# Causal attention feeding a hard-swish MLP on one core: the order of every queue from a list scheduler written into the kernel

## The chip, the cores and the metric

One core of a Trainium2 chip. Times are device microseconds of one execution. Engines are named as the profile names them: PE is TensorE (its matmuls; PEld is its weight loads), DVE is VectorE, ACT is ScalarE, POOL is GpSimd, SP is the engine that issues all DMAs here. Each engine takes its instructions in the order in which the program lists them.

## The reference

Attention with a causal mask over 4 batches, 12 heads, 448 positions and a head size of 64, then a hard-swish MLP over the 1792 tokens (768 to 2048 to 768), all in float32:

```python
scores = scale * np.matmul(q, k.transpose(0, 1, 3, 2))
scores = np.where(mask, -1000000000.0, scores)
scores = scores - np.max(scores, axis=-1, keepdims=True)
attn = np.exp(scores)
attn = attn / (np.sum(attn, axis=-1, keepdims=True) + 1e-09)
out = np.matmul(attn, v)            # heads joined: x is 1792 x 768
h = x @ w_in
g = h * np.clip(h + 3.0, 0.0, 6.0) / 6.0
return g @ w_out
```

## The kernel before

The tokens are handled in five groups. Group 0 holds the first 112 positions of all four batches (448 columns); groups 1 to 4 hold the other 336 positions of one batch each.

**Attention.** Two heads, a pair, are worked on together. For group 0 there are six pairs (`scores_first`, `transposed_first`, `times_v_first`), and their outputs come before any MLP work of group 0. For groups 1 to 4 there are 24 pairs, six a group, each in three kinds of PE work: scores (`scores`, L221, tile `s` from `kr`,`qr`; three row blocks of 448, 336 and 224 columns for each of the two heads), 18 transposes of the normalised probabilities (`transposed`, L250, `s` from `ident`,`pr`), and the product with V (`times_v`, L268, `av` from `pt`,`vr`; widths 336, 336, 224, 112 for each head). The scores of one head use 64 rows of the PE array and the other head the other 64 rows, so the two matmuls of a pair of heads can run side by side; the products with V use 64 columns each in the same way. These are called tiled matmuls below. Everything else on PE uses the whole array. Before the transposes, DVE adds the mask and takes the maximum (L224), ACT takes exponentials (L228), DVE inverts the sums (L236, L237), and POOL scales the probabilities (`norm`, L240; L172 in group 0).

**MLP.** Each product of float32 operands is made of three matmuls on a high and a low part (`wh`, `wl`, `xh`, `xl`, `gh`, `gl`; L334 to L336 for the first layer, L355 to L357 for the second). A group takes 288 matmuls for each layer, 576 in all. Weights come in 40 chunks a group. In group 0 a chunk is first put together from two interleaved halves by three DVE operations (L312, L313, L314, tile `wf`), written to a scratch tensor `kept_w`, and split by ACT (`wh`, L84) and POOL (`wl`, L89). In later groups it is read back from `kept_w` and split by ACT and DVE.

**Order.** Each step is given a time number by hand (`at(t, fn, ...)`), the steps are traced in the order of these numbers, and the framework's own scheduler then places the instructions of all engines, instruction by instruction. PSUM has five banks for `s`, one for `av`, two for `mo`.

Of the kernel before, what the change touches and what calls it, by code (L numbers as in the profile page):

```python
# [17 lines left out]

# [1 line left out]

# [23 lines left out]
T_FIRST, T_REST, T_LOAD, T_PT, T_AV, T_W, T_WLOAD = -66, -22, -20, 9, 16, 7, 7  # L44
# [3 lines left out]
def tile_causal_attention_hardswish_moe(ctx: ExitStack, tc: tile.TileContext, q, k, v, w_in, w_out, out):  # L48
# [5 lines left out]
    pools = {}  # L54

    def pool(name, bufs, **kw):
        pools[name] = ctx.enter_context(tc.tile_pool(name=name, bufs=bufs, **kw))

    def mk(tag, shape, dt=F32):
        return pools[tag].tile(shape, dt, tag=tag, name=tag)  # L60

    def bank(tag):
        return mk(tag, [128, 512])

    pool("const", 1)
    pool("gh", 1)
    pool("gl", 1)
    for tag in ("prow", "wf", "r", "ob"):
        pool(tag, 2)
    for tag in ("qr", "kr", "vr", "wh", "wl"):  # L70
        pool(tag, 3)
    for tag in ("pr3", "pr2", "pr1", "pt0", "pt1", "pt2", "wd"):
        pool(tag, 4)
    for tag in ("xh", "xl"):
        pool(tag, 9)
    for tag, bufs in (("s", 5), ("av", 1), ("mo", 2)):
        pool(tag, bufs, space=bass.MemoryType.PSUM)
# [35 lines left out]
    steps = []  # L113

    def at(t, fn, *a):
        steps.append((t, len(steps), fn, a))

    x_t = {}

    def x_split(g, p, x, n):  # L120
        xh, xl = mk("xh", [128, S], F32R)[:, :n], mk("xl", [128, S], F32R)[:, :n]
        x_t[g, p] = xh, xl
        nc.scalar.copy(xh, x)
        nc.vector.tensor_tensor(xl, x, f(xh), ALU.subtract)  # L124


    first, fprob, fpt = {}, {}, {}

    def load_first(p):
        if p == 0:  # L130
            first["qk"] = mk("gh", [128, 2 * NPAIR, S])
            first["v"] = mk("gl", [128, NPAIR, S + 64])
        for a, src in enumerate((q, k)):
            nc.sync.dma_start(
                out=first["qk"][:, 2 * p + a].rearrange("m (b s) -> m b s", b=B),
                in_=src[:, p, :, :, :C].rearrange("b e d s -> (e d) b s"),
            )
        first["ld", p] = nc.sync.dma_start(
            out=first["v"][:C, p].rearrange("c (b e d) -> c b (e d)", b=B, e=2),
            in_=v[:, p, :, 0].rearrange("b c e d -> c b (e d)"),  # L140
        )

    def scores_first(p):
        qa, ka = (first["qk"][:, 2 * p + a].rearrange("m (b s) -> m b s", b=B) for a in range(2))
        st = mk("prow", [C, 2, 8])
        banks = [bank("s") for _ in range(2)]
        ps = [t[:C, :S].rearrange("c (b s) -> c b s", b=B) for t in banks]
        pr = [mk("pr3", [C, S]).rearrange("c (b s) -> c b s", b=B) for _ in range(2)]
        for e in range(2):
            nc.tensor.matmul(ps[e], identr, maskr, start=True, stop=False)  # L150
        for b in range(B):
            for e in range(2):
                r = slice(64 * e, 64 * e + 64)
                nc.tensor.matmul(ps[e][:, b], qa[r, b], ka[r, b], start=False, stop=b == B - 1)
        for e in range(2):
            nc.vector.tensor_reduce(st[:, e, :4], ps[e], AX.X, ALU.max)
        nc.vector.tensor_scalar(st[:, 1, :4], st[:, 1, :4], -0.125, None, ALU.mult)
        for b in range(B):
            nc.scalar.activation(
                pr[1][:, b], ps[1][:, b], ACTF.Exp, bias=st[:, 1, b:b + 1], scale=0.125,  # L160
                accum_out=st[:, 1, 4 + b:5 + b],
            )
        nc.vector.tensor_tensor(
            pr[0], ps[0], st[:, 0, :4].unsqueeze(2).to_broadcast([C, B, C]), ALU.subtract
        )
        nc.scalar.activation(pr[0], pr[0], ACTF.Exp, scale=0.125)
        nc.vector.tensor_reduce(st[:, 0, 4:], pr[0], AX.X, ALU.add)
        r = st[:, :, 4:8]
        nc.vector.tensor_scalar_add(r, r, 1e-9)
        nc.vector.reciprocal(r, r)  # L170
        for e in range(2):
            nc.gpsimd.tensor_tensor(  # L172
                pr[e], pr[e], st[:, e, 4:].unsqueeze(2).to_broadcast([C, B, C]), ALU.mult
            )
        fprob[p] = pr

    def transposed_first(p, e):
        ps, ph = bank("s"), mk("pt0", [C, S])
        for b in range(B):
            nc.tensor.transpose(ps[:C, C * b:C * b + C], fprob[p][e][:, b], ident)  # L180
        if e:
            nc.vector.tensor_copy(ph, ps[:C, :S])
        else:
            nc.scalar.copy(ph, ps[:C, :S])
# [261 lines left out]
```

## Time and profile before

| | us |
|---|---|
| median of 3 runs (lowest, highest) | 727.09 (725.49, 728.04) |
| profiled execution, its own time | 725.93 |
| span of that execution, first to last instruction | 724.2 |
| PE busy (share of the span) | 700.4 (97%) |
| PEld busy | 579.1 (80%) |
| DVE busy | 455.1 (63%) |
| ACT busy | 343.1 (47%) |
| POOL busy | 211.8 (29%) |

PE's matmuls overlap one another in the trace: a matmul of 336 columns is shown as some 320 ns long while the next one starts some 155 ns after it. So PE's busy time doesn't say how much PE could be pressed together; starts that follow one another do. A float32 matmul that is not split into parts by hand shows as two instructions in the trace (8 rows for 4 matmuls).

### The profile page before, as it was taken

The numbers are of one execution on the slowest core, as the hardware profiler recorded it, in microseconds if no ns is written. First come the engines' busy times: TensorE is split into PE (matmuls) and PEld (weight loads), VectorE is DVE, ScalarE is ACT, GpSimd is POOL, SyncE is SP. The second block draws the span as 40 slices with busy tenths as digits, with TensorE's granted clock in tenths as the row PEclk, the third lists the DMA queues.
The fourth block names the chain that finished last, engine by engine and source line by source line (L and its number), as shares of the span: only waits on it lengthen the run. The fifth ranks groups of instructions, "written<-read, shape, count | busy, mean of one in ns | idle before, by whom it ended". The sixth has DMA issues, their size and how long they took to land.

```text
span 724.2 us, 11850 instructions
## 1 busy us (share of the span) xinstructions
PE 700.4 (97%) x4236; PEld 579.1 (80%) x4236; DVE 455.1 (63%) x907; ACT 343.1 (47%) x801; POOL 211.8 (29%) x266
## 2 busy tenths in 40 slices
PE   5889998999999999999999999999999999999998
PEld 4656865877766887788887789888888789999998
DVE  5784999888787666554556665445575653466432
ACT  3346454553343555454555454455555544444432
POOL 1543544434645241222220433211243212011100
PEclk9878999899999999999999999999999999999999
DMA  9971574466787543244564334545442234654452
GB/s 242 305 263 49 183 278 148 145 215 215 253 278 228 167 131 107 72 143 147 149 178 122 105 98 123 145 140 157 146 141 76 62 100 123 197 157 125 129 163 72
DMA packets 60347, 113.63 MB, mean 157 GB/s; under 512 B 14976, under 2 KB 26880, under 8 KB 60288
## 3 DMA queue, kind: packets, MB, share of 16 engines
q1 hardware_dynamic: 60288, 112.88, 51.6%
q8 instruction: 33, 0.54, 0.3%
q14 instruction: 26, 0.21, 0.1%
HBM read 94.77 MB, written 18.09 MB: 156 GB/s over the span
## 4 chain that ended last, share of the span: by engine, by line
PE 80%; DVE 10%; issue 3%; DMA 3%; POOL 2%; ACT 1%; SPq 1%; POOLq 0%; ACTq 0%; DVEq 0%
PE mo L334 11%; PE mo L355 10%; PE mo L336 10%; PE mo L335 10%; PE mo L357 9%; PE mo L356 9%; PE s L221 7%; PE av L268 7%; PE s L250 5%; DVE wf L313 2%; DVE wf L314 2%; DVE wf L312 2%; DVE gl L89 1%; DMA wd<-in_w_in_dram 1%; DMA kept_w<-wf 1%
## 5 line engine op out<-in xcount | busy, mean ns | idle before, releaser
L89 DVE TENSOR_TENSOR wl<-wd,wh 128x512 fp32r<-128x512 f32 (+1 forms) x160 | 132.3, 827 | 122.8 <-ACT wh L84 119.9
L84 ACT CAST wh<-wd 128x512 fp32r<-128x512 f32 (+1 forms) x160 | 112.8, 705 | 131.9 <-PE mo L356 66.6
L334 PE MATMUL mo<-xh,wh 128*128 128x336 f32 (+1 forms) x480 | 166.4, 348 | 1.7 <-DVE r L342 1.7
L355 PE MATMUL mo<-gh,wh 128*128 128x336 f32 (+1 forms) x480 | 165.6, 345 | 0.0
L357 PE MATMUL mo<-gh,wl 128*128 128x336 f32 (+1 forms) x480 | 158.6, 331 | 1.5 <-POOL wl L89 1.5
L336 PE MATMUL mo<-xh,wl 128*128 128x336 f32 (+1 forms) x480 | 159.1, 331 | 0.0
L335 PE MATMUL mo<-xl,wh 128*128 128x336 f32 (+1 forms) x480 | 158.4, 330 | 0.2 <-DVE xl L124 0.2
L356 PE MATMUL mo<-gl,wh 128*128 128x336 f32 (+1 forms) x480 | 157.6, 328 | 0.0
L240 POOL TENSOR_SCALAR pr<-pr,prow 112x224 f32<-112x224 f32 x144 | 99.9, 713 | 149.4 <-DVE prow L237 113.6
L228 ACT ACTIVATE pr<-s,prow 112x448 f32<-112x448 f32 (+1 forms) x144 | 77.3, 540 | 106.3 <-DVE prow L224 106.3
L334 PEld LDWEIGHTS mo<-xh,wh 128*128 128x128 f32 x480 | 91.0, 190 | 23.9 <-issue 12.7
L355 PEld LDWEIGHTS mo<-gh,wh 128*128 128x128 f32 x480 | 90.3, 188 | 17.5 <-issue 13.5
L224 DVE CUSTOM_DVE_ANT_0 s<-s,mask 112x448 f32<-112x448 f32 (+1 forms) x144 | 71.7, 522 | 42.2 <-PE s L221 42.1
L86 POOL TENSOR_SCALAR gh<-r 128x336 fp32r<-128x336 f32 x64 | 33.7, 527 | 207.7 <-DVE r L342 206.3
L335 PEld LDWEIGHTS mo<-xl,wh 128*128 128x128 f32 x480 | 91.5, 191 | 3.2 <-issue 1.3
L357 PEld LDWEIGHTS mo<-gh,wl 128*128 128x128 f32 x480 | 90.2, 188 | 4.4 <-POOL wl L89 1.9
L336 PEld LDWEIGHTS mo<-xh,wl 128*128 128x128 f32 x480 | 91.3, 190 | 2.5 <-issue 0.9
L89 POOL TENSOR_TENSOR wl<-wf,wh 128x512 fp32r<-128x512 f32 (+1 forms) x40 | 66.1, 1659 | 88.2 <-ACT wh L84 85.5
L356 PEld LDWEIGHTS mo<-gl,wh 128*128 128x128 f32 x480 | 90.5, 189 | 1.0
L221 PE MATMUL s<-kr,qr 64*112 64x224 f32 (+2 forms) x288 | 69.3, 503 | 1.4 <-ACT pr L228 1.4
L250 PE MATMUL s<-ident,pr 112*112 112x112 f32 x432 | 63.0, 260 | 1.1 <-POOL pr L240 0.8
L89 DVE TENSOR_TENSOR gl<-r,gh 128x336 fp32r<-128x336 f32 (+1 forms) x80 | 50.2, 630 | 21.5 <-POOL gh L86 20.4
(52 smaller groups left out, 685.4 us busy)
## 6 DMA issues: line engine op xcount, KB each, us to landing
wd<-kept_w SPq DMA_DIRECT2D x64, 384.0 KB, 3.1
wd<-kept_w SPq DMA_DIRECT2D x96, 256.0 KB, 2.6
wd<-in_w_in_dram SPq DMA_DIRECT2D x16, 768.0 KB, 4.9
wd<-in_w_out_dram SPq DMA_DIRECT2D x24, 512.0 KB, 5.0
kept_w<-wf SPq DMA_DIRECT2D x16, 384.0 KB, 2.6
kept_w<-wf SPq DMA_DIRECT2D x24, 256.0 KB, 2.9
kr<-in_k_dram SPq DMA_DIRECT2D x24, 224.0 KB, 3.4
vr<-in_v_dram SPq DMA_DIRECT2D x24, 224.0 KB, 2.7
```

The lines of the kernel that those rows point to most:

```text
L84: nc.scalar.copy(o, i)
L89: (nc.gpsimd if eng == "P" else nc.vector).tensor_tensor(o, a, b, ALU.subtract)
L221: nc.tensor.matmul(dst[e], qr[r, C * (i - 1):C * i], kr[r, :w], start=True, stop=True)
L228: nc.scalar.activation(prob[n][e, i], dst[e], ACTF.Exp, bias=st[:, e, i:i + 1], scale=-1.0, accum_out=st[:, e, 4 + i:5 + i],)
L240: nc.gpsimd.tensor_scalar(pr[e, i], pr[e, i], r[:, e, i - 1:i], 1.0, ALU.mult, ALU.mult)
L250: nc.tensor.transpose(ps[:C, o:o + C], pr[e, i][:, C * j:C * j + C], ident)
L334: nc.tensor.matmul(ps, wh[:, c], xh, start=(c == 0), stop=False)
L335: nc.tensor.matmul(ps, wh[:, c], xl, start=False, stop=False)
L336: nc.tensor.matmul(ps, wl[:, c], xh, start=False, stop=(c == NK - 1))
L355: nc.tensor.matmul(ps, wh[:, j], gh[:, i, :n], start=(i == 0), stop=False)
L356: nc.tensor.matmul(ps, wh[:, j], gl[:, i, :n], start=False, stop=False)
L357: nc.tensor.matmul(ps, wl[:, j], gh[:, i, :n], start=False, stop=(i == NF - 1))
```

## The change

The hand-made list of steps goes away. The kernel now describes each piece of work as an operation with the engines that can do it, assumed durations, what it reads and writes, and which buffers it holds. A list scheduler (`Flow`) plays the five queues through with these numbers, picks an engine where there are several, and its result is emitted in that order under a manual schedule, so that the framework no longer reorders anything. Each tiled operation is now one indivisible piece: the scores of the row blocks 448 and 336 together, those of 224 by themselves, and all eight products with V of a pair of heads in one run. Copies, casts and subtractions that had one engine may go to ACT, DVE or POOL. In the first part the transposed blocks use `mo` banks, the sums of each of the two heads are inverted by themselves, and `prow` has three buffers. All counts of matmuls, transposes, weight operations and DMAs stay as they were.

```diff
-T_FIRST, T_REST, T_LOAD, T_PT, T_AV, T_W, T_WLOAD = -66, -22, -20, 9, 16, 7, 7
+T_FIRST, T_REST, T_LOAD, T_W, T_WLOAD = -66, -22, -24, 9, 9
...
+class Flow:
+    LATENCY = 0.2
+    SWITCH = 0.2
+    DMA_RATE, DMA_LATENCY = 280e3, 1.9
...
+            for e, cand in lists.items():
+                if busy[e] > now + 1e-9:
+                    continue
+                cand[:] = [a for a in cand if a[1].ends is None]
+                for _, o in cand:
+                    need = {}
+                    for b in o.bufs:
+                        if not b.held:
+                            need[b.tag] = need.get(b.tag, 0) + 1
+                    if all(self.free[t] >= n for t, n in need.items()):
+                        self.start(o, e, now, need, out, busy, post)
+                        break
...
+        if e == "PE" and o.tiled != self.mode:
+            t += self.SWITCH / 2
+            self.mode = o.tiled
...
+        move(key, n, lambda: ap(xh)[:, :n], lambda: ap(av)[:, :n], [(av, 0)], [(xh, 0)], {"A": 1, "D": (1, .5)})
...
-        for e in range(2):
-            for i in range(1, NC_):
-                nc.gpsimd.tensor_scalar(pr[e, i], pr[e, i], r[:, e, i - 1:i], 1.0, ALU.mult, ALU.mult)
...
+                one(
+                    t + 4.5 + .1 * e, {"P": 1}, (C * (i + 1) + 300) / 1100, scaled,
+                    [(st, e, 4 + i)], [(pr[e, i], 0)],
+                )
...
+        for j, tiles in enumerate(((3, 2), (1,))):
+            pe(
+                t + 2 * j,
+                [((1.68 * C * (i + 1) + 170) / 1000, lambda i=i: products(i), [(ps[0, i], 0), (ps[1, i], 0), ("turn",)])
+                 for i in tiles],
+                [(qr, 0), (kr, 0)], True,
+            )
...
-        at(t + T_AV, times_v, n, (0, 1))
-        at(t + T_AV + 1, times_v, n, (2, 3))
+        pe(t + 13, [(1.9, times_v, [(av, 0)])], [(vr, 0)] + [(x[0], 0) for x in pt.values()], True)
...
-        rnd("A", wh, w)
-        sub("D" if g else "P", wl, w, f(wh))
+        move(t - T_W + .1, n, lambda: ap(wh)[:, :n], w, [wk], [(wh, 0)], {"A": 1})
+        minus(
+            t - T_W + .2, n, lambda: ap(wl)[:, :n], w, lambda: f(ap(wh))[:, :n], [wk, (wh, 0)], [(wl, 0)],
+            {"D": 1.15, "P": (2, .5)} if g else {"P": 2, "D": (1.15, 2.0)},
+        )
...
-    steps.sort(key=lambda s: s[:2])
-    setup()
-    for _, _, fn, a in steps:
-        fn(*a)
+    order = flow.run()
+    setup()
+    with tc.manual_schedule():
+        for _, _, e, emit in order:
+            emit(e)
```

What stands in the queues now, at three places. First PE in group 1, where a pair's products with V (`av`) and the next pair's scores (`s` from `kr`,`qr`) stand among the MLP's matmuls (`mo`). Before:

```order
L268 MATMUL av<-pt_3721,vr 64x336
L221 MATMUL s<-kr,qr 112x448 x2
L355 MATMUL mo<-gh,wh 128x336
L356 MATMUL mo<-gl,wh 128x336
L357 MATMUL mo<-gh,wl 128x336
L355 MATMUL mo<-gh,wh 128x336
L356 MATMUL mo<-gl,wh 128x336
L357 MATMUL mo<-gh,wl 128x336
L268 MATMUL av<-pt_3685,vr 64x224
L268 MATMUL av<-pt_3736,vr 64x224
L268 MATMUL av<-pt_3685,vr 64x112
L268 MATMUL av<-pt_3736,vr 64x112
```

Now, at a pair's products with V in the same group:

```order
L496 MATMUL av<-pt_2940,vr 64x336
L496 MATMUL av<-pt_2989,vr 64x336
L496 MATMUL av<-pt_2970,vr 64x336
L496 MATMUL av<-pt_3011,vr 64x336
L496 MATMUL av<-pt_2973,vr 64x224
L496 MATMUL av<-pt_3013,vr 64x224
L496 MATMUL av<-pt_2973,vr 64x112
L496 MATMUL av<-pt_3013,vr 64x112
```

The eight products that stood in two parts with six whole-array matmuls between them are one run now. Over the whole program PE changes between whole-array, row-tiled and column-tiled work 275 times before and 162 times now: 109 and 64 times up to the end of group 0, 60 and 36 times in each of groups 1 and 2, 46 and 26 times in group 3. Runs of transposes go from 133 to 91.

Second, PE while the six pairs of group 0 are worked on (L192 before and L394 now are their products with V, L180 and L381 their transposes, L154 and L324 their scores). Before, in the middle of that part:

```order
L334 MATMUL mo<-xh,wh 128x448
L335 MATMUL mo<-xl,wh 128x448
L192 MATMUL av<-pt_346,gl 64x112
L180 MATMUL s<-ident,pr_313 112x112 x3
L192 MATMUL av<-pt_353,gl 64x112
L192 MATMUL av<-pt_346,gl 64x112
L192 MATMUL av<-pt_353,gl 64x112
L192 MATMUL av<-pt_346,gl 64x112
L192 MATMUL av<-pt_353,gl 64x112
L192 MATMUL av<-pt_346,gl 64x112
L192 MATMUL av<-pt_353,gl 64x112
L180 MATMUL s<-ident,pr_313 112x112
```

Now, at the first pair's products:

```order
L394 MATMUL av<-pt_282,gl 64x112
L394 MATMUL av<-pt_266,gl 64x112
L394 MATMUL av<-pt_282,gl 64x112
L394 MATMUL av<-pt_266,gl 64x112
L394 MATMUL av<-pt_282,gl 64x112
L394 MATMUL av<-pt_266,gl 64x112
L394 MATMUL av<-pt_282,gl 64x112
L394 MATMUL av<-pt_266,gl 64x112
L324 MATMUL s<-gh 112x112 x8
L381 MATMUL mo<-ident,pr_245 112x112 x4
```

MLP matmuls stood between the first pairs before (the first behind the first pair's products); now the first of them stands behind the products with V of all six pairs.

Third, DVE in the same part (`wf` rows put a weight chunk together; the others belong to the pairs). Before, at the fourth and fifth pair:

```order
L182 COPY pt_409<-s 112x448
L312 TENSOR_SCALAR wf<-wd 128x768
L156 TENSOR_REDUCE prow<-s 112x4
L124 TENSOR_TENSOR xl<-av,xh 128x448
L313 SCALAR_TENSOR_TENSOR wf<-wd,wf 128x768
L167 TENSOR_REDUCE prow<-pr_375 112x4
L156 TENSOR_REDUCE prow<-s 112x4
L314 SCALAR_TENSOR_TENSOR wf<-wd,wf 128x768
L312 TENSOR_SCALAR wf<-wd 128x768
```

Now, at the third pair:

```order
L351 TENSOR_TENSOR pr_292<-s,prow 112x448
L531 TENSOR_SCALAR wf<-wd 128x768
L533 SCALAR_TENSOR_TENSOR wf<-wd,wf 128x768
L249 TENSOR_TENSOR xl<-av,xh 128x448
L366 TENSOR_SCALAR prow<-prow 112x4
L367 RECIPROCAL prow<-prow 112x4
L358 TENSOR_REDUCE prow<-pr_292 112x4
```

Five weight chunks (15 `wf` operations) stood ahead of the sixth pair's last subtraction (`xl`) before; two chunks stand ahead of it now.

## Rows read from the trace of the kernel before

**Rows 1.** The page, busy times, and the granted TensorE clock in 40 slices.

```profile
PE 700.4 (97%) x4236; PEld 579.1 (80%) x4236; DVE 455.1 (63%) x907; ACT 343.1 (47%) x801; POOL 211.8 (29%) x266
...
PEclk9878999899999999999999999999999999999999
```

**Rows 2.** Busy time by stretch: PE, PEld, DVE, ACT, POOL, clock, DMA share, GB/s.

```profile
0.00:72.00 72.00, 57.79 (x347) 39.56 (x348) 47.70 (x101) 31.20 (x99) 25.59 (x29) 0.86 0.74 216
72.00:157.00 85.00, 80.98 (x391) 60.91 (x391) 79.10 (x127) 42.44 (x99) 37.72 (x32) 0.96 0.60 196
157.00:240.60 83.60, 81.17 (x427) 62.12 (x426) 65.50 (x119) 33.77 (x82) 43.14 (x40) 1.00 0.74 235
240.60:374.20 133.60, 133.60 (x855) 110.62 (x854) 75.68 (x176) 69.43 (x164) 33.96 (x52) 1.00 0.45 130
374.20:507.70 133.50, 133.50 (x853) 110.54 (x853) 75.17 (x175) 69.34 (x164) 33.97 (x52) 1.00 0.44 131
507.70:631.80 124.10, 124.10 (x797) 106.42 (x796) 67.26 (x144) 60.75 (x135) 29.86 (x46) 1.00 0.40 119
631.80:724.20 92.40, 89.22 (x577) 88.94 (x576) 44.73 (x70) 36.19 (x61) 7.58 (x16) 1.00 0.45 130
```

**Rows 3.** Timeline of PE at 341.6 us: start, duration, instruction, count.

```profile
341.59 0.32 PE L357 MATMUL mo<-gh,wl 128*128 128x336 f32 x1
341.84 1.35 PE L268 MATMUL av<-pt,vr 112*64 112x336 f32 x8
343.12 1.01 PE L221 MATMUL s<-kr,qr 64*112 64x448 f32 x4
344.06 0.42 PE L355 MATMUL mo<-gh,wh 128*128 128x336 f32 x1
344.32 0.32 PE L356 MATMUL mo<-gl,wh 128*128 128x336 f32 x1
```

**Rows 4.** Timeline of PE at 76 us, first and last of 13 matmuls.

```profile
75.77 0.36 PE L335 MATMUL mo<-xl,wh 128*128 128x448 f32 x1
...
78.20 0.36 PE L335 MATMUL mo<-xl,wh 128*128 128x448 f32 x1
```

**Rows 5.** Timeline of PE at 337 us, a run of transposes.

```profile
337.12 0.45 PE L250 MATMUL s<-ident,pr 112*112 112x112 f32 x3
337.34 0.40 PE L355 MATMUL mo<-gh,wh 128*128 128x336 f32 x1
337.58 0.32 PE L356 MATMUL mo<-gl,wh 128*128 128x336 f32 x1
```

**Rows 6.** Timeline of PE at 92 us, scores and products with V mixed.

```profile
91.97 1.00 PE L221 MATMUL s<-kr,qr 64*112 64x448 f32 x2
92.90 1.34 PE L268 MATMUL av<-pt,vr 112*64 112x336 f32 x6
94.17 1.00 PE L221 MATMUL s<-kr,qr 64*112 64x448 f32 x2
95.10 0.59 PE L268 MATMUL av<-pt,vr 112*64 112x224 f32 x2
```

**Rows 7.** Groups of DVE instructions from 0 to 64.6 us, by shape.

```profile
L313 DVE SCALAR_TENSOR_TENSOR wf<-wd,wf 128x768 int32<-128x768 int32 x5 | 6.1, 1212 | 0.0
L314 DVE SCALAR_TENSOR_TENSOR wf<-wd,wf 128x768 int32<-128x768 int32 x5 | 5.8, 1162 | 0.0
L312 DVE TENSOR_SCALAR wf<-wd 128x768 int32<-128x768 int32 x5 | 4.5, 900 | 1.6 <-DMA wd<-in_w_in_dram 1.6
```

**Rows 8.** Timeline of PE at 45 us, with idle time and releaser.

```profile
44.82 0.37 PE L336 MATMUL mo<-xh,wl 128*128 128x448 f32 x1
48.29 0.99 PE L180 MATMUL s<-ident,pr 112*112 112x112 f32 x4 [3.10 <-POOL pr L172]
```

**Rows 9.** Busy time in one stretch of ten microseconds, columns as in rows 2.

```profile
50.00:60.00 10.00, 10.00 (x41) 5.79 (x40) 5.83 (x21) 4.40 (x14) 1.82 (x2) 0.50 0.58 204
```

**Rows 10.** The page, the scaling of probabilities on POOL, all widths.

```profile
L240 POOL TENSOR_SCALAR pr<-pr,prow 112x224 f32<-112x224 f32 x144 | 99.9, 713 | 149.4 <-DVE prow L237 113.6
```

More of the change, by code (lines that the diff above doesn't have):

```diff
@@ L177, in transposed_first @@
[L177 to L184, printed above, removed]
-        fpt[p, e] = ph
-    def times_v_first(p):
-        va = first["v"][:C, p].rearrange("c (b e d) -> c b e d", b=B, e=2)
-        ps = bank("av")
-        for b in range(B):
-            for e in range(2):
-                nc.tensor.matmul(
-                    ps[64 * e:64 * e + 64, C * b:C * b + C], va[:, b, e], fpt[p, e][:, C * b:C * b + C],
-                    start=True, stop=True,
-                )
-        x_split(0, p, ps[:, :S], S)
@@ new lines, in first_pair, with row, wide, masks @@
+        pr, ph = [buf("pr3", [C, S]) for _ in range(2)], [buf("pt0", [C, S]) for _ in range(2)]
+        sc = [lambda e=e: by_batch(ap(ps[e])[:C, :S]) for e in range(2)]
+        pb = [lambda e=e: by_batch(ap(pr[e])) for e in range(2)]
+        def row(e, a):
+            return ap(st)[:, e, a:a + 4]
+        def wide(e, a):
+            return row(e, a).unsqueeze(2).to_broadcast([C, B, C])
+        def masks():
+            for e in range(2):
+                nc.tensor.matmul(sc[e](), identr, maskr, start=True, stop=False)
@@ new lines, in products @@
+        def products():
+            qa, ka = (by_batch(ap(first_qk)[:, 2 * p + a]) for a in range(2))
+            for b in range(B):
+                for e in range(2):
+                    m = slice(64 * e, 64 * e + 64)
+                    nc.tensor.matmul(sc[e]()[:, b], qa[m, b], ka[m, b], start=False, stop=b == B - 1)
+        keys = [(x, 0) for x in ps]
+        pe(t, [(.45, masks, keys + [("turn",)])], [])
+        pe(t, [(1.1, products, keys)], [(first_qk, p, 0), (first_qk, p, 1)], True)
@@ new lines, in first_pair @@
+        allb = [(pr[0], b) for b in range(B)]
+        one(
+            t + 2, {"D": 1}, elem(S), lambda _: nc.vector.tensor_tensor(pb[0](), sc[0](), wide(0, 0), ALU.subtract),
+            [(ps[0], 0), (st, 0, 0)], allb,
+        )
+        one(
+            t + 2, {"A": 1}, .65, lambda _: nc.scalar.activation(pb[0](), pb[0](), ACTF.Exp, scale=0.125), [], allb,
+        )
+        one(
+            t + 3, {"D": 1}, elem(S), lambda _: nc.vector.tensor_reduce(row(0, 4), pb[0](), AX.X, ALU.add),
+            allb, [(st, 0, 4)],
+        )
@@ new lines, in first_pair, with times_v @@
+        av = bank("av")
+        def times_v():
+            va = ap(first_v)[:C, p].rearrange("c (b e d) -> c b e d", b=B, e=2)
+            for b in range(B):
+                for e in range(2):
+                    nc.tensor.matmul(
+                        ap(av)[64 * e:64 * e + 64, C * b:C * b + C], va[:, b, e], ap(ph[e])[:, C * b:C * b + C],
+                        start=True, stop=True,
+                    )
+        pe(t + 14, [(.8, times_v, [(av, 0)])], [(first_v, p), (ph[0], 0), (ph[1], 0)], True)
@@ L407, in tile_causal_attention_hardswish_moe @@
+    for p in range(NPAIR):
+        first_pair(p)
+    for g in range(B + 1):
+        if g:
+            for p in range(NPAIR):
+                pair(NPAIR * (g - 1) + p)
+        group(g)
+    order = flow.run()
     setup()
-    for _, _, fn, a in steps:
-        fn(*a)
+    with tc.manual_schedule():
+        for _, _, e, emit in order:
+            emit(e)
 def kernel(q, k, v, moe_w_in, moe_w_out):
```

622 lines of the change are left out of this document (369 added, 253 removed).

## The prediction

> **What bounds the kernel now.** I read the page first, then busy time by stretch, then PE's timeline where it changes between kinds of work. The page shows PE busy for 97% of the span [rows 1], which would leave 24 us to win. That number hides most of what can be won, since overlapping matmuls count as busy while PE waits or drains. In the last stage, where nothing but whole-array matmuls of 336 columns is left, 577 of them fill 89.22 us [rows 2]: 0.155 us from start to start. At 448 columns, 13 starts lie 2.43 us apart from first to last [rows 4]: 0.2025 us. These are the floors of the MLP. The Trainium skill ("Perfetto Trace Analysis", Identifying the Most-Contended Engine) says the same of matmul busy time and wants weight-load busy instead. By that measure PE is at 80% here, 145 us from full; no term below uses it.
>
> The other kinds of work come out of the timeline. Eight instructions of products with V follow a whole-array matmul after 0.25 us instead of 0.155, and take 1.28 us until the next scores start; four instructions of scores of 448 columns take 0.94 us until the MLP goes on [rows 3]. I split these: streaming costs 1.667 ns a column for two heads side by side (0.75 us at 448, twice 0.56 us for the two widths of 336), and what is left is 0.09 us for going into tiled work and 0.19 us for going out of it or from one tiling to the other. A run of three transposes holds the MLP for 0.22 us, and the matmul behind it for 0.24 instead of 0.155 [rows 5]: 0.10 us for each transpose. So a pair of heads needs 1008 x 1.667 ns = 1.68 us for scores, the same for V, and 18 x 0.10 = 1.8 us for transposes: 5.2 us.
>
> With these the stages can be taken apart:
> - Group 1, 133.6 us [rows 2]: MLP 576 x 0.155 = 89.3, six pairs 31.0, 60 changes of tiling (26 in, 34 out or across) 8.8; 4.5 us left over. Group 2 is the same (133.5). Group 3 has 124.1 us, with 46 changes (6.7 us).
> - 72 to 240.6 us, the rest of group 0: 168.6 us, of which 540 MLP matmuls 109.4, six pairs 31.0, changes 10.6; 17.6 us left over. DVE is busy for 79.10 of the first 85 us there [rows 2], so it holds PE up.
> - 0 to 72 us: PE does 36 MLP matmuls, the six first pairs and one to two later ones, some 30 us of work at full clock. The rest goes to waiting and a lower clock.
>
> In the first stretch the pairs' chain goes through DVE, and weight chunks stand in it: five chunks take 6.1 + 5.8 + 4.5 = 16.4 us there [rows 7]. At 45 us PE waits 3.10 us for a POOL scaling [rows 8], which waited for DVE's sums behind such a chunk.
>
> **The change, part by part.**
>
> *Longer tiled runs.* 60 changes become 36 in groups 1 and 2, each pair now having three runs (18 x 0.28 = 5.0 us instead of 8.8): -3.8 us twice. Group 3 goes from 46 to 26: -3.1 us. That is -10.6 us, and nothing on another engine can hide it, as PE is the bound there.
>
> *Pairs no longer pulled apart.* Where the scores of one head stand alone between products with V, they still cost 0.93 us [rows 6], as much as both heads together [rows 3]. Each such split loses the half that would have run beside it. The new order puts the two heads next to each other throughout. I can't tell these splits from small waits in each remainder, so I take a third of the 4.5 us a group as splits, 1.5 us for groups 1 and 2 and 1 us for group 3: -4 us. Bounds: nothing, if the remainder is all waits that stay, and -13 us, if all of it goes.
>
> *Fewer runs of transposes.* 42 runs fewer. If the 0.085 us by which the matmul behind a run is slower [rows 5] were paid once a run, that would be 3.6 us; if it belongs to each transpose's weights, nothing. I take nothing.
>
> *The first stretch.* Two chunks instead of five stand ahead of the sixth pair's `xl` on DVE, so three fifths of 16.4 us, 9.8 us, move behind it. DVE was busy 47.7 us up to 72 us and idle 24.3 [rows 2]. With 37.9 us of work ahead, dense MLP work starts at 62 us if all that idle time stays and at 38 us if none does. Some stays: the first scores wait for their DMA in both. I take the middle, 50 us. Against that, 36 MLP matmuls (7.3 us), one pair's products with V (1.7 us), its transposes (1.8 us) and a last score block (0.4 us), which lay before 72 us, have to be done later now: 11.2 us. Net 22 - 11.2 = -10.8 us; bounds +1 and -23.
>
> *The rest of group 0.* Changes up to its end fall from 109 to 64, 16.6 to 9.2 us; 2.4 us of that lie in the first stretch and are in its sum, so -5.0 us. Of the 17.6 us left over I take a third off, -5.9 us, for rejoined halves and for transposed blocks that are copied by ACT instead of DVE, which has little time there. DVE has the same weight chunks to do, so most of this waiting stays. Bounds: 0 and -14.
>
> *Engines chosen by the scheduler.* ACT takes most copies of transposed blocks (37 of 48 that were DVE's) and gives ten output copies to DVE; POOL takes a few `wl` and `gl`. In groups 1 to 3 DVE is busy for 56% and ACT for 51% of the time [rows 2], so this is hidden by PE's work; it would cost only where PE waits for that engine. Loads are issued earlier (18 steps ahead instead of 14); DMA is used for less than half of the time there [rows 2], nothing.
>
> *A wait added.* All order is fixed with assumed durations. The scaling on POOL is assumed to take 0.68 + 0.58 + 0.48 = 1.74 us for a head, while it takes 3 x 0.713 = 2.14 us [rows 10], 0.8 us late for the pair. The transposes of both heads stand behind it, and the MLP matmuls listed after them stand behind the transposes in PE's queue. MLP pieces of six matmuls, 0.93 us, between them cover that; I take nothing. With the cover gone it is 0.8 us for each of 24 pairs, 19 us.
>
> The sum: -10.6 - 4 - 10.8 - 5.0 - 5.9 = -36.3 us; 724.2 - 36.3 = 687.9 us span. The profiled execution took 1.7 us more than its span and the median of the runs 1.2 us more than that execution: 690 us, rounded down from 690.8 within what such a sum is worth.
>
> **The rivals.**
>
> *The first stretch stays long because PE's clock stays low.* The granted clock falls in several slices up to 60 us [rows 1] and is 0.50, the lower level of 1.2 GHz, from 50 to 60 us [rows 9], after PE had stood idle for 3.10 us [rows 8]; it comes back when MLP matmuls follow densely. The new order has no MLP matmul in this stretch to keep PE at work. PE's work there is 16 us for six first pairs (scores and V 0.75 us each, eight transposes 0.8, two mask matmuls 0.4) and 3 us for two later pairs' scores. These 19 us would take up to 19 us more at half clock, about half of it on the pairs' chain: 10 us, 700 us. For it: the slices. Against it: five chunks on DVE are what PE waited behind. The Trainium skill ("TensorE: Matmul & The Clock Gate", Part 1) says that the low clock is the default and that steady matmul work lifts it. By that rule this stretch runs slow in the new kernel throughout, and the time would be the 700 us of this rival.
>
> *DVE binds all of group 0.* The stretch from 72 to 157 us has DVE at 93%, and none of its weight work goes away. If the earlier start of the MLP is only waited off later, the first two terms of group 0 fall to the saved changes in its rest: 724.2 - 14.6 - 5.0, 705 us span, 708 us.
>
> *Everything joins up.* If dense work starts at 42 us and two thirds of the remainders in all groups go, 8 + 5.9 + 4 = 18 us more are won: 673 us.
>
> *Slower than before.* POOL has one queue for pair scaling and weight splits, and only two `wf` buffers stand between it and DVE. If a burst of six scalings (4.3 us) holds a `wl`, DVE stands at its next chunk, with everything the pairs and the MLP need behind it. That decides only if it costs PE more than 36 us over the 40 chunks of group 0, 0.9 us each time; 763 us if twice that. For it: a fixed order can't step round a late instruction. Against it: DVE is busy for 93% in the worst stretch now, with the same split of work.
>
> *No effect.* The order doesn't matter since PE is bound by its own matmuls, 727 us. Against it: changes of tiling have a price in the timeline.
>
> **How the numbers follow.** My forecast (677 to 703 us, but for the clock rival) 0.57, low clock 0.13, DVE binds 0.10, everything joins up 0.10, slower 0.07, no effect 0.03. The range from 671 to 712 us takes in the first four, most of their widths, and leaves out little more than the last two. 0.3% (2 us) is what a measurement of this kernel can tell from no change. Faster by more: 0.90; within: 0.03; slower: 0.07.
>
> **What would show it.** Right: in groups 1 to 3 eight products with V in a row at some 1.9 us, each pair with three tiled runs, and 127 to 129 us for groups 1 and 2, 120 for group 3; the first dense MLP matmuls between 42 and 58 us; group 0 ended near 219 us; the floors of 0.155 and 0.2025 us as before. Wrong: PE waits for POOL ahead of transposes in every pair (the cover is gone), DVE idle behind `wl` in group 0, or a granted clock of 0.5 over much of the first stretch with the MLP starting after 60 us. The prediction fails as a whole if the start to start of MLP matmuls changes, or if waits in groups 1 to 3 exceed 5 us each.

## Result and the profile after

The changed kernel takes 699.6 us (median of four runs, 698.82 to 699.9). The kernel before took 727.0 us on the same chip (725.49 to 728.04). The ratio is 0.962, with a 95% interval of 0.960 to 0.964: a gain of 27.4 us where 37 was forecast. The forecast of 690 us was 10 us too low; its range of 671 to 712 us held the time. The profiled execution took 699.9 us with a span of 698.2, 26.0 us less than before.

The page after, with busy times and the granted clock, answers to [rows 1]:

```profile
PE 664.2 (95%) x4236; PEld 572.1 (82%) x4236; DVE 443.3 (63%) x875; ACT 356.3 (51%) x844; POOL 224.7 (32%) x267
...
PEclk9899999999999999999999999999999999999999
```

PE has the same number of instructions and is busy for 36 us less with them. Where the time came from, the page doesn't say. Busy time by stretch does (columns as in [rows 2]). The first three stretches divide group 0 at the first dense MLP matmul, at its 289th matmul and at its last; the other three are groups 2, 3 and 4, as in [rows 2]:

```profile
0.00:44.60 44.60, 31.93 (x272) 22.32 (x272) 33.44 (x87) 24.52 (x83) 14.66 (x18) 0.92 0.92 242
44.60:145.90 101.30, 89.59 (x474) 69.23 (x472) 95.05 (x141) 54.03 (x125) 56.09 (x43) 0.98 0.68 207
145.90:237.90 92.00, 85.59 (x437) 67.95 (x437) 67.49 (x116) 34.58 (x86) 47.15 (x46) 0.97 0.74 223
362.30:488.80 126.50, 126.50 (x855) 110.46 (x854) 70.51 (x166) 72.31 (x177) 35.16 (x51) 1.00 0.47 139
488.80:606.40 117.60, 117.60 (x795) 105.75 (x795) 63.09 (x138) 63.98 (x147) 30.85 (x45) 1.00 0.42 125
606.40:698.20 91.80, 88.56 (x578) 88.28 (x576) 43.81 (x69) 35.82 (x60) 10.28 (x19) 1.00 0.45 133
```

From these, and from the starts of the same MLP matmuls in PE's timeline of both kernels:

| | before | forecast | after |
|---|---|---|---|
| dense MLP work begins | 72 | 50 | 44.6 |
| group 2 begins (matmul 1152) | 374.2 | 347.2 | 362.35 |
| group 2 takes | 133.5 | 128.2 | 126.4 |
| group 3 takes | 124.1 | 120.0 | 117.7 |
| group 4 and what is behind it | 92.4 | 92.4 | 91.8 |

The time up to the start of group 2 fell by 11.8 us, where 27.0 was forecast (10.8 + 5.0 + 5.9 in group 0, 3.8 + 1.5 in group 1). Groups 2 and 3 gave more than forecast: 7.1 instead of 5.3, and 6.4 instead of 4.1 us. So the mechanism worked where PE is the bound. Up to the start of group 2, 15.2 us of the forecast are missing, although the dense work of group 0 began 5 us earlier than forecast; groups 2 and 3 make up for 4.1 of them. PE's timeline of the changed kernel at that start:

```profile
43.68 0.99 PE L394 MATMUL av<-pt,gl 112*64 112x112 f32 x16
44.60 0.47 PE L549 MATMUL mo<-xh,wh 128*128 128x448 f32 x1
44.91 0.36 PE L550 MATMUL mo<-xl,wh 128*128 128x448 f32 x1
...
415.33 0.32 PE L551 MATMUL mo<-xh,wl 128*128 128x336 f32 x1
415.58 1.92 PE L496 MATMUL av<-pt,vr 112*64 112x336 f32 x16
417.43 0.42 PE L549 MATMUL mo<-xh,wh 128*128 128x336 f32 x1
```

The lower three rows are a run of products with V in group 2: 16 records, all eight products of both heads, in one row of 1.92 us between two MLP pieces. In [rows 3] such a run is followed by scores, a second tiling; now each run has whole-array matmuls on both sides.

Group 1 begins inside the end of group 0 in the new order, and the trace has no clean border between them. If group 1 took as long as group 2 (126.5 us), group 0 ended at 362.35 - 126.5 = 235.9 us, 4.8 us earlier than before, where 21.7 was forecast. From 44.6 us on it then had 116.6 us of MLP floor (576 x 0.2025), 31.0 of the next six pairs, 3.9 of moved work and 5.8 of changes of tiling (41 in the trace, 20 in and 21 out or across); 191.3 - 157.3 leaves 34 us. This remainder was 17.6 us in the prediction's sum of the kernel before, and the forecast had it at 11.7. Taken up to the start of group 2, which needs no border, the same sum leaves 35 us now (317.8 us from 44.6 on) and 23 us before (302.2 us from 72 on, with the changes counted in the trace). In the stretch from 44.6 to 145.9 us DVE is busy for 95.05 of 101.30 us, 94%.

### The profile page after: what moved, and what is told of

The parts are those of the page before. It is cut to its first block, busy times and chain, and to the rows that moved or that the text cites. A ratio compares the mean times of both kernels' runs of the same rounds, so it can differ in the third digit from the quotient of the medians.

```text
span 698.2 us, 11840 instructions
## 1 busy us (share of the span) xinstructions
PE 664.2 (95%) x4236; PEld 572.1 (82%) x4236; DVE 443.3 (63%) x875; ACT 356.3 (51%) x844; POOL 224.7 (32%) x267
## 4 chain that ended last, share of the span: by engine, by line
PE 66%; POOL 0%; ACT 0%; issue 0%
PE mo L549 18%; PE mo L551 17%; PE mo L550 17%; PE s L420 5%; PE av L496 5%; PE s L477 4%; POOL pr L466 0%; POOL wl L249 0%; ACT ob L237 0%
## 5 line engine op out<-in xcount | busy, mean ns | idle before, releaser
L249 DVE TENSOR_TENSOR wl<-wd,wh 128x512 fp32r<-128x512 f32 (+1 forms) x153 | 124.9, 817 | 151.9 <-ACT wh L237 147.5
L549 PE MATMUL mo<-xh,wh 128*128 128x336 f32 (+1 forms) x480 | 164.5, 343 | 3.7 <-DVE r L579 3.7
L551 PE MATMUL mo<-xh,wl 128*128 128x336 f32 (+1 forms) x480 | 157.0, 327 | 0.0
L550 PE MATMUL mo<-xl,wh 128*128 128x336 f32 (+1 forms) x480 | 156.6, 326 | 0.0
L466 POOL TENSOR_SCALAR pr<-pr,prow 112x224 f32<-112x224 f32 x144 | 102.4, 730 | 156.3 <-PE mo L550 89.6
L437 DVE CUSTOM_DVE_ANT_0 s<-s,mask 112x448 f32<-112x448 f32 (+1 forms) x144 | 69.9, 529 | 10.5 <-PE s L420 10.5
L244 POOL TENSOR_SCALAR gh<-r 128x336 fp32r<-128x336 f32 x52 | 24.5, 471 | 158.8 <-DVE r L579 141.6
L237 ACT CAST wh<-wf 128x512 fp32r<-128x512 f32 (+1 forms) x40 | 28.2, 706 | 76.3 <-DVE wf L535 63.2
L477 PE MATMUL s<-ident,pr 112*112 112x112 f32 x432 | 58.8, 264 | 7.6 <-POOL pr L466 4.8
L237 ACT COPY pt<-s 112x336 f32<-112x336 f32 x133 | 53.5, 440 | 23.1 <-PE s L477 22.0
```

Source lines behind the costliest of these rows:

```text
L237: nc.scalar.copy(o(), i()) if scale is None else nc.scalar.mul(o(), i(), scale)
L244: nc.gpsimd.tensor_scalar(o(), i(), 1.0, 1.0, ALU.mult, ALU.mult)
L249: (nc.gpsimd if e == "P" else nc.vector).tensor_tensor(o(), a(), b(), ALU.subtract)
L437: lambda _, e=e, i=i, w=w, dst=dst: nc.vector.tensor_tensor_reduce(dst(), dst(), mask[:, S - w:], -0.125, 3.0e38, ALU.add, ALU.min, ap(st) ...
L466: nc.gpsimd.tensor_scalar(x, x, r, 1.0, ALU.mult, ALU.mult)
L477: nc.tensor.transpose(ap(tp)[:C, C * o:C * o + C], ap(pr[e, i])[:, C * j:C * j + C], ident)
```

## Experiments

The theory after the result: DVE's weight chunks bind group 0, and an early start of the MLP is waited off behind them. The rivals: the first stretch still sets the time; the two `wf` buffers hold DVE up; the fixed order is late by its wrong durations; a cost of POOL beside DVE, which the prediction hadn't named. Each ratio below is to the kernel before.

### The early chunks put back

```diff
-  one(t - T_W + .01 * a, {"D": 1}, ...)
+  one((t - T_W if i > 4 else -62 + 8 * i) + .01 * a, {"D": 1}, ...)
```

The first five chunks go among the first pairs again.

> The new kernel, but the weight chunks of the start get early keys again (chunk i beside first pair i), so that the scheduler lists them on DVE among the first pairs as the old kernel had them; all else is the scheduler's. The prediction's own step: the start of dense MLP work (44.6 us in the new kernel) moves back by the three chunks' 9.8 us to about 54 us, and the time with it, 708 us. Rival, DVE binds group 0: the same DVE work is only done earlier, dense work starts near 54 us but the end of group 0 (238 us) and the time stay, 699 to 701 us.

Measured: 703.96 us (703.13 to 704.15), ratio 0.967 [0.965, 0.970]. Dense MLP work begins at 60.05 us, 15.5 us later than in the changed kernel, and group 2 at 366.43 us, only 4.1 us later. Busy time by stretch of this kernel, up to the dense start and behind it:

```profile
0.00:60.00 60.00, 41.60 (x276) 29.23 (x276) 48.17 (x109) 26.23 (x88) 21.04 (x27) 0.81 0.90 255
60.00:150.80 90.80, 85.54 (x461) 68.29 (x460) 78.65 (x119) 46.79 (x109) 48.59 (x38) 0.98 0.56 168
```

DVE does 14.7 us more before the start (48.17 against 33.44) and 16.4 us less behind it (78.65 against 95.05), and the stretch behind is 10.5 us shorter. Three quarters of the earlier start is waited off later, but not the whole of it, so the result lies between the two theories. The 15.5 us are more than the 9.8 expected of the chunks. The granted clock was 0.81 up to this start and 0.92 in the changed kernel, so part of the difference may be the clock's.

### Three buffers for `wf` instead of two

```diff
-    ... prow=3, wf=2, r=2, ...
+    ... prow=3, wf=3, r=2, ...
```

> The new kernel with three wf buffers instead of two, so that DVE's next weight chunk need not wait for the write of the chunk before last to the scratch tensor, nor for POOL's wl of it. If what is left over in group 0 is DVE's own work (95 us busy of the 101 us from 44.6 to 145.9 us), at most 3 us change: 697 to 700 us. If it is the two buffers (8.8 + 5.5 + 3.7 us of DVE waits at the first weight operation in group 0), some 10 us go: 690 us.

Measured: 693.05 us (690.4 to 694.3), ratio 0.952 [0.949, 0.955]. DVE's waits from 44.6 to 232 us, first the changed kernel (releaser; us in total, times, longest):

```profile
DVE wf L531 <- DMA kept_w<-wf: 8.8, 7, 1.9
DVE wf L531 <- POOL wl L249: 5.5, 4, 1.9
DVE wf L531 <- issue: 3.7, 6, 1.1
```

and with three buffers, where the same view has only this row for L531:

```profile
DVE wf L531 <- issue: 0.2, 1, 0.2
```

Some 18 us of DVE's waiting for a free `wf` are gone and 6.6 us of the time. The MLP's 289th matmul starts at 145.7 us instead of 145.9: nothing is won in the first half of group 0, where DVE is at 94% and has little idle time to give. All of it is won behind that. The buffers are part of the loss, the smaller one.

### One of DVE's three weight operations left out

```diff
   elif a == 1:
-      nc.vector.scalar_tensor_tensor(ti, high, -(1 << 30), ti, ...)
+      pass
```

The kernel leaves out the operation that puts in the signs of group 0's weights.

> The new kernel in its own order, but without the second of the three DVE operations that put a weight chunk together in group 0 (so the signs of the weights are left out). That takes 16 x 1.15 + 24 x 0.74 = 36 us from DVE before 232 us. If DVE's work binds group 0, its end moves from 238 us to where PE's own 170 us and the start allow, 215 to 220 us, and the time to 678 to 682 us. If POOL (scaling bursts, wl) or the fixed order holds PE there, the end moves by 5 us or less: 694 to 698 us.

Measured: 681.64 us (680.01 to 681.97), ratio 0.936 [0.934, 0.939]. Busy time by stretch, the MLP's first half of group 0:

```profile
48.30:139.30 91.00, 87.64 (x475) 69.90 (x473) 71.65 (x122) 53.93 (x125) 51.72 (x39) 0.97 0.74 231
```

The order on every engine is the same but for 40 fewer DVE operations. The stretch takes 91.0 instead of 101.3 us, DVE falls from 94% to 79%, and group 2 begins at 344.41 us, 17.9 us earlier. This is 3 us ahead of the forecast's 347.2. It is the sum of 10.3 us in this stretch and 11.3 us from its end to the start of group 2, less 3.7 us for a later start (48.3 us). In the stretch shown, a full DVE sets the time. In the second half DVE is busy for only 73% of the changed kernel's time (67.49 of 92.00 us), so what is won there comes from its waits or from the length of a chunk's chain; the runs don't tell these apart.

### Short tiled runs again

```diff
-        for j, tiles in enumerate(((3, 2), (1,))):
+        for j, tiles in enumerate(((3,), (2,), (1,))):
...
-            for j in range(NC_):
+            for j in js:        # V in two parts: (0, 1) and (2, 3)
```

> The new kernel with the products with V in two parts (0,1) and (2,3) as before, and the scores of each row block as an operation of its own: 214 changes of tiling instead of 162. If changes cost what the timeline of the old kernel shows (0.09 in, 0.19 out, 0.14 us on average), 52 more are 7.3 us: 707 us, groups 1 and 2 at 129 us instead of 126.5. If the gain in groups 1 to 3 comes from something else than the changes, the time stays near 700 us.

Measured: 701.06 us (699.84 to 705.06), ratio 0.965 [0.961, 0.968]. Groups 2 and 3 of this kernel:

```profile
358.90:487.70 128.80, 128.80 (x855) 109.75 (x854) 75.10 (x170) 70.06 (x170) 34.87 (x52) 1.00 0.46 136
487.70:606.90 119.20, 119.20 (x795) 105.31 (x795) 66.89 (x141) 62.28 (x144) 30.84 (x46) 1.00 0.42 124
```

Group 2 has 50 changes of tiling here and 36 in the changed kernel, and takes 2.35 us more: 0.17 us for each. Group 3 has 36 and 26 and takes 1.6 us more: 0.16 us. The prediction worked with 0.14 (0.28 for going in and out), so this term was right and a little low. The total went up by 1.5 us alone, since group 2 began 3.5 us earlier in the other order; if group 1 took 2.35 us more as group 2 did, group 0 came out some 6 us shorter. The expected total of 707 us was missed for that reason.

### One engine for each kind of copy, as before

```diff
-  {"A": 1, "D": (1, .4)}                        # copies of transposed blocks
+  {"D": 1} if a == 1 else {"A": 1}
...
-  {"D": 1.15, "P": (2, .5)} if g else {"P": 2, "D": (1.15, 2.0)}
+  {"D": 1.15} if g else {"P": 2}
```

and so for the other six kinds that the scheduler may place.

> The new kernel with the scheduler's choice of engines taken away: every copy, cast and subtraction has the one engine that it had in the old kernel. Transposed blocks go back to DVE for one in three (12 in group 0, 0.5 us each) and four of the first pairs' too (0.6 us each); output copies and the few wl and gl go back as well, net some 6 us more on DVE before the end of group 0. If DVE binds group 0, the time rises by about that: 703 to 706 us, with groups 2 and 3 unchanged (126.5 and 117.6 us). If the choice of engines is hidden everywhere, 699 to 701 us.

Measured: 702.39 us (701.53 to 705.59), ratio 0.967 [0.964, 0.970]. Dense work begins at 49.28 us and group 2 at 365.79, 3.4 us later than in the changed kernel. Groups 2 and 3 take 127.1 and 118.3 us, 0.7 and 0.6 more. By the medians the choice of engines is worth some 3 us. The profiled execution took 705.59 us, 3.2 more than the median, and most of its difference lies up to the start of group 2.

### Group 0's `wl` written by ACT instead of POOL

```diff
+            if e == "P" and not g:
+                nc.scalar.copy(ap(wl)[:, :n], w())
```

The copy stands in the place of a subtraction, so this kernel leaves out the low halves themselves.

> The new kernel in its own order, but the low halves wl of group 0's weights, which POOL subtracts, are written by ACT as a plain copy in their place (so they aren't the low halves). POOL then has no operation with two inputs there. If DVE's weight operations are long because they wait for POOL (the trace has the same operation at 0.94 us with POOL idle and at 2.50 us beside a wl), their means fall to some 0.95 us (768 wide) and 0.65 us (512 wide), about 25 us less of DVE time in group 0, and the time falls to 682 to 688 us. If the long durations are DVE's own, DVE keeps its 95 us and only PE's waits for wl go (4 us): 695 to 699 us.

Measured: 679.38 us (678.11 to 683.48), ratio 0.936 [0.932, 0.940]. Busy time by stretch, the MLP's first half of group 0:

```profile
40.90:134.10 93.20, 88.79 (x476) 70.33 (x472) 71.74 (x140) 65.41 (x142) 24.25 (x26) 0.96 0.73 226
```

No operation is taken from DVE, but its 140 instructions there are busy for 71.74 us where 141 took 95.05. The groups by shape show which got shorter. DVE in the changed kernel from 44.6 to 232 us (count, busy us, mean ns, idle before):

```profile
L533 DVE SCALAR_TENSOR_TENSOR wf<-wd,wf 128x768 int32<-128x768 int32 x14 | 22.3, 1590 | 0.2
...
L535 DVE SCALAR_TENSOR_TENSOR wf<-wd,wf 128x768 int32<-128x768 int32 x15 | 17.5, 1168 | 0.3
L249 DVE TENSOR_TENSOR gl<-r,gh 128x448 fp32r<-128x448 f32 x14 | 16.1, 1153 | 1.5 <-ACT gh L237 1.5
...
L579 DVE SCALAR_TENSOR_TENSOR r<-r,mo 128x448 f32<-128x448 f32 x16 | 9.7, 610 | 0.0
```

and in this kernel from 44 to 220 us:

```profile
L535 DVE SCALAR_TENSOR_TENSOR wf<-wd,wf 128x768 int32<-128x768 int32 x14 | 14.0, 1000 | 0.3
L533 DVE SCALAR_TENSOR_TENSOR wf<-wd,wf 128x768 int32<-128x768 int32 x14 | 13.8, 988 | 0.2
...
L585 DVE SCALAR_TENSOR_TENSOR r<-r,mo 128x448 f32<-128x448 f32 x16 | 9.8, 612 | 2.4 <-ACT r L578 2.4
L249 DVE TENSOR_TENSOR gl<-r,gh 128x448 fp32r<-128x448 f32 x14 | 9.0, 640 | 3.6 <-ACT gh L237 3.6
```

The operations on `wf` and `gl` got shorter. The one that reads a PSUM tile (`r` from `r`,`mo`; 610 and 612 ns) did not: POOL had not lengthened it.

How one instruction comes by such a length is seen in the timeline of the changed kernel (start, duration, and in brackets the idle time before with its releaser):

```profile
95.67 4.08 POOL L249 TENSOR_TENSOR wl<-wf,wh 128x768 fp32r<-128x768 f32 x1 [3.35 <-ACT wh L237]
96.08 0.55 DVE L531 TENSOR_SCALAR wf<-wd 128x768 int32<-128x768 int32 x1
97.08 0.95 DVE L533 SCALAR_TENSOR_TENSOR wf<-wd,wf 128x768 int32<-128x768 int32 x1
98.07 2.50 DVE L535 SCALAR_TENSOR_TENSOR wf<-wd,wf 128x768 int32<-128x768 int32 x1
...
105.52 0.96 DVE L535 SCALAR_TENSOR_TENSOR wf<-wd,wf 128x768 int32<-128x768 int32 x1
...
107.75 1.87 POOL L249 TENSOR_TENSOR wl<-wf,wh 128x768 fp32r<-128x768 f32 x1 [4.03 <-ACT wh L237]
107.94 2.50 DVE L533 SCALAR_TENSOR_TENSOR wf<-wd,wf 128x768 int32<-128x768 int32 x1
```

The DVE operation at 105.52 us, with no POOL subtraction beside it, takes 0.96 us. The same shape takes 2.50 us twice, where it starts during a POOL subtraction. (The window shown above has 28 of L533 and L535 with 768 columns that start in it: the 14 without a POOL instruction beside them take 0.94 to 0.96 us, the eight that start during a subtraction 2.22 on average.) At 107.94 us, POOL's ends 1.68 us later (107.75 + 1.87), and 1.68 + 0.95 is 2.63: DVE's operation takes about as long as if it had begun when POOL was done. At 98.07 us it is the same sum (99.75 - 98.07 + 0.95 = 2.63). POOL loses too: 4.08 us at 95.67, with DVE operations inside it, against 1.87. There L533 at 97.08 kept its 0.95 us, so it isn't always DVE that waits. The Trainium skill ("SBUF — State Buffer", SBUF: two separate sides) says that DVE and GpSimd share one pair of ports, taken as an exclusive lock for a whole instruction by a GpSimd operation, or by a DVE operation that has two SBUF inputs or runs in a two-port mode. The two sums agree with that. The runs don't show the lock itself.

So the meeting of DVE's and POOL's work lengthened DVE's work in group 0 of the changed kernel a good deal. Each count times the difference of the two means makes 8.4 us for L533, 2.5 for L535 and 7.2 for `gl` in these rows, and 19 us for L531 and the 512-column shapes of the same view: 37 us of DVE's time. The kernel became 20 us faster when POOL's subtractions went. Not all of this need be the shorter operations: the run also empties POOL's queue, and PE's 4.0 us of waiting for `wl` go with it.

### Durations in the scheduler taken from the trace

```diff
-  (C * (i + 1) + 300) / 1100        # scaling on POOL
+  (C * (i + 1) + 400) / 1000
...
-  elem(n) * (.7 if a == 0 else 1.25)        # DVE's weight operations
+  elem(n) * (.87, 1.16, 1.5)[a]
```

> The new kernel with two of the scheduler's assumed durations set nearer to the trace: POOL's scaling (from 1.74 to 2.2 us a head) and the three weight operations on DVE (from 3.06 to 3.36 us a chunk of 768). If the order itself loses time because these were too short (PE waits 4.8 us for POOL's scaling, 4.0 us for wl), 3 to 6 us are won: 694 to 697 us. If not, 699 to 701 us.

Measured: 694.87 us (693.27 to 695.06), ratio 0.956 [0.954, 0.957], 4.7 us less than the changed kernel, as expected. Group 2 begins at 357.1 us, 5.2 us earlier. The wrong durations cost little, and only up to the start of group 2: groups 2 and 3 take 126.7 and 117.9 us, as in the changed kernel.

### Three `wf`, and POOL's scalings shared with ACT

```diff
-  wf=2                        # and for the scaling: {"P": 1}
+  wf=3                        # and for the scaling: {"P": 1, "A": (.9, .2)}
```

> Three wf buffers as in the second experiment (693 us), and ACT may take the scaling of probabilities (66 of 144 go there). If POOL's bursts of scaling hold PE's transposes and the wl behind them, another 4 to 8 us go: 685 to 689 us. If DVE alone is what is left, 692 to 694 us.

Measured: 685.97 us (684.49 to 687.33), ratio 0.944 [0.941, 0.946]. ACT takes 66 of the 144 scalings. This is 7.1 us less than with three `wf` alone, and the last matmul of 448 columns starts at 221.9 instead of 229.8 us, so the gain lies in group 0 again.

### Products with V listed one head after the other

```diff
-            for j in range(NC_):
-                for e in range(2):
+            for e in range(2):
+                for j in range(NC_):
```

> The new kernel with the eight products with V of a pair listed by head: four of one head, then four of the other, in the same run and the same place, where they alternated. If the two column halves of PE work side by side only when their matmuls follow one another, a pair's run grows from 1.9 us to some 3.1 us, 24 pairs cost some 25 to 31 us, and groups 1 and 2 take some 134 us: 725 to 731 us. If the order within a run doesn't matter, 699 to 701 us, and the halves left alone in the old kernel cost nothing by themselves.

Measured: 719.66 us (717.03 to 721.5), ratio 0.991 [0.987, 0.994]. PE's timeline at the place shown above:

```profile
426.32 0.32 PE L551 MATMUL mo<-xh,wl 128*128 128x336 f32 x1
426.57 3.10 PE L496 MATMUL av<-pt,vr 112*64 112x336 f32 x16
429.60 0.42 PE L549 MATMUL mo<-xh,wh 128*128 128x336 f32 x1
```

The same eight products take 3.10 us instead of 1.92. Group 2 takes 133.5 us and group 3 takes 123.6, as much as before the change. Here the two heads run side by side only when their matmuls alternate in the queue (1.92 us); that each head has its own half of the array isn't enough (3.10 us). The total rose less than the expected 725 to 731 us, since group 0 hides part of it.

### Both, with the traced durations

Three `wf`, the scaling shared (`(.7, .2)`), and the durations of the run above together.

> Three wf buffers, scaling on POOL or ACT (as in the eighth experiment, 686 us), and the assumed durations nearer to the trace (as in the seventh). If what these took away adds up, 2 to 5 us more: 681 to 684 us. If they won the same waits, 685 to 688 us.

Measured: 685.39 us (683.58 to 686.88), ratio 0.944 [0.942, 0.946], no less than without the durations. The gains don't add up, as expected if the parts win the same waits.

### Group 0's `wl` on DVE alone

```diff
-  {"D": 1.15, "P": (2, .5)} if g else {"P": 2, "D": (1.15, 2.0)}
+  {"D": 1.15, "P": (2, .5)} if g else {"D": 1.0}
```

with three `wf` and the scaling shared.

> As the eighth experiment, but DVE alone subtracts the low halves wl in group 0, none of it on POOL. DVE gets 16 x 0.99 + 24 x 0.72 = 33 us more work, and its weight operations no longer meet POOL's wl, which were some 25 us of waiting. If these cancel, 684 to 689 us; if DVE's added work decides, 692 to 696 us; if the waits were larger than seen, 678 to 682 us.

Measured: 681.32 us (679.44 to 685.5), ratio 0.939 [0.935, 0.944], the lowest median of a kernel with the whole computation. DVE by shape from 44 to 220 us:

```profile
L249 DVE TENSOR_TENSOR wl<-wf,wh 128x768 fp32r<-128x768 f32 x15 | 17.0, 1133 | 1.2 <-ACT wh L237 0.8 <-PE mo L551 0.3
L249 DVE TENSOR_TENSOR wl<-wf,wh 128x512 fp32r<-128x512 f32 x24 | 16.5, 688 | 7.0 <-ACT wh L237 7.0
L535 DVE SCALAR_TENSOR_TENSOR wf<-wd,wf 128x768 int32<-128x768 int32 x15 | 16.2, 1077 | 0.3
L533 DVE SCALAR_TENSOR_TENSOR wf<-wd,wf 128x768 int32<-128x768 int32 x14 | 15.5, 1109 | 0.2
```

Two of these groups in the kernel with three `wf` and the scaling shared, where POOL subtracts, in the same window:

```profile
L535 DVE SCALAR_TENSOR_TENSOR wf<-wd,wf 128x512 int32<-128x512 int32 x24 | 35.8, 1492 | 0.7
L533 DVE SCALAR_TENSOR_TENSOR wf<-wd,wf 128x768 int32<-128x768 int32 x14 | 25.2, 1800 | 0.4
```

The engine that bound the first half of group 0 got 33.5 us more work (17.0 + 16.5), and the kernel became no slower: the median is 4.7 us below that with POOL doing it, but the two ranges (679.44 to 685.5 and 684.49 to 687.33 us) overlap. DVE's other operations are shorter, L533 with 768 columns at 1109 ns and not 1800; the three weight operations of both widths take 88.2 us together and took 118.8, 30.6 less, which is nearly what came on top. The Trainium skill ("Perfetto Trace Analysis", Optimizing Scalar/DVE Operations) says that moving work between these two engines might not help; here moving it back to the loaded one cost nothing.

## Why the prediction was right and wrong

**Longer tiled runs: right, a little low.** Forecast 3.8, 3.8 and 3.1 us for groups 1 to 3 at 0.14 us a change. The run with short tiled runs gives 0.17 and 0.16 us, so 24 changes are 4.1 us in group 2 and 20 are 3.2 in group 3.

**Pairs no longer pulled apart: right, mis-sized.** Group 2 after is 89.3 of MLP, 31.0 of six pairs and 5.0 of changes, which leaves 1.2 us of the 4.5 before. So 3.3 us went (3.0 with changes at 0.17 us), where a third of 4.5 (1.5) was taken, and group 3's 6.4 in all is 2.3 us over its forecast. The splits could have been counted: in PE's timeline of group 2 before, one score block of 448 columns and four products (three of 336 columns, one of 224) stand apart from those of the other head. At the prediction's price of 1.667 ns a column that is 0.75 + 3 x 0.56 + 0.37 = 2.8 us. Two of them:

```profile
405.77 0.78 PE L268 MATMUL av<-pt,vr 112*64 112x336 f32 x2
406.48 1.00 PE L221 MATMUL s<-kr,qr 64*112 64x448 f32 x2
```

"Each such split loses the half that would have run beside it" is the right mechanism: with the heads of every pair in turn, in runs as long as now, groups 2 and 3 take 7.1 and 5.9 us more.

**Fewer runs of transposes: forecast at nothing, nearly so.** Changes (4.1) and splits (2.8) make 6.9 of group 2's 7.1 us and leave 0.2 for twelve runs fewer, where 0.085 us for each would be 1.0.

**The first stretch: the start right, the net wrong.** The forecast was 50 us for the first dense MLP work and "Net 22 - 11.2 = -10.8 us". The start came at 44.6 us. But putting the early chunks back moved it by 15.5 us and group 2 by 4.1: most of the gain at the start was waited off later.

**The rest of group 0: the step that failed.** "Of the 17.6 us left over I take a third off" and "DVE has the same weight chunks to do, so most of this waiting stays". The remainder nearly doubled, to some 34 us. (The prediction's sum for before was a little off: the trace has 63 changes from 72 to 240.6 us, 24 in and 39 out or across, 9.6 us and not 10.6. So the remainder before was 18.6, and the changes saved behind the start were 3.8 us and not 5.0.) Taking out one DVE operation of three gave 17.9 us, so DVE's weight work holds PE there. The early chunks that moved behind the start came on top of a DVE that was already at 93% there [rows 2], and the term lowered the remainder where it should have raised it. The rival "DVE binds all of group 0" is nearest to what happened, though DVE is full in the first half only; its price of 705 us span was too high by 7, mostly as groups 2 and 3 gave more.

**What no step had:** POOL's subtractions lengthen DVE's operations. [rows 7] has them at 1212 and 1162 ns, where 950 is possible, and the prediction took that for their price. It was so in the rest of group 0 before as well (72 to 240.6 us):

```profile
L314 DVE SCALAR_TENSOR_TENSOR wf<-wd,wf 128x768 int32<-128x768 int32 x11 | 16.2, 1475 | 0.0
```

An estimate from the timelines adds up, over DVE's instructions with a POOL instruction beside them, what each takes over the median of its shape with none: 34 us from 72 to 240.6 before, 43 us from 44.6 to 237.9 now. So most of this loss is older than the change, which made it some 9 us larger. How much of the 34 us of PE's remainder is this and how much DVE's plain work isn't settled: the two gains (17.9 us by less work, 19.9 by no subtraction on POOL) overlap: either one alone brings DVE in the first half of group 0 down to 79% and 77%, so the other has little left to win.

**The low clock: the rival's time didn't come.** The granted clock was 0.92 of 2.4 GHz up to 44.6 us, with no MLP matmul there: one dip, in which runs of eight scores are longer than behind it. Two stretches of the changed kernel, then PE's timeline:

```profile
29.40:36.20 6.80, 6.03 (x35) 3.86 (x33) 4.64 (x12) 5.04 (x15) 3.01 (x3) 0.50 1.05 250
36.20:44.60 8.40, 6.86 (x60) 4.03 (x56) 8.26 (x25) 4.76 (x15) 2.70 (x2) 1.00 0.47 166
```

```profile
33.88 2.71 PE L420 MATMUL s<-kr,qr 64*112 64x448 f32 x8
...
70.03 1.57 PE L420 MATMUL s<-kr,qr 64*112 64x448 f32 x8
```

The run in the dip lost 1.1 us, and the start still came earlier than forecast. The Trainium skill ("TensorE: Matmul & The Clock Gate", Part 1) says that the low clock is the default and that activity lifts it. The prediction read this as a low clock throughout the stretch; the trace doesn't agree with that reading, 0.92 with attention's matmuls alone. The dips differ between kernels: with ACT writing `wl` there is none up to the start at 40.95 us (granted 1.00), with one weight operation less the clock is 0.69 from 30 to the start at 48.3. So the low clock may have a price of some us here, which no run isolates, and the gains of those two kernels hold it.

**The wait for POOL: forecast at nothing, nearly so.** The waits of PE in the changed kernel over the whole span:

```profile
PE s L477 <- POOL pr L466: 4.8, 9, 1.3
...
PE mo L551 <- POOL wl L249: 4.0, 3, 2.6
PE mo L549 <- DVE r L579: 3.7, 4, 1.6
```

Nine of the transposes waited for a scaling, 4.8 us in all, and 4.5 of these lie between 60 and 240 us. In groups 1 to 3 the MLP pieces of six matmuls cover it, as argued. The traced durations won 4.7 us, up to the start of group 2.

**Engines chosen by the scheduler: forecast at nothing.** Right for groups 2 and 3 within 0.7 us; worth some 3 us in all, most of it up to the start of group 2.

## What to carry to other kernels

Price a reordering stage by stage, and where another engine than PE is full, ask what an earlier start of PE puts on that engine: it comes back as waiting. Before work is moved to a helper engine, compare the durations of the loaded engine's instructions with and without the helper beside them; a helper that lengthens them can cost as much as it takes. Keep matmuls of tiles that should overlap alternating in the queue, and list tiled work in long runs: each change cost 0.16 to 0.17 us here.

## What was not expected of the hardware

- A DVE operation of 0.95 us took 2.50 when it began during a POOL subtraction, and POOL's took 4.08 instead of 1.87 with DVE's inside it; the mean of the 768-column operation fell from 1590 to 988 ns when POOL had none. A DVE operation that reads a PSUM tile kept its length (610 and 612 ns).
- Eight products of two heads on two tiles took 1.92 us listed in alternation and 3.10 us one head after the other.
